# Performer attention and MLP: chunks of six token tiles with 384-column seven-product matmuls in place of chunks of four with 256- and 512-column ones

## The chip, the cores and the metric

The kernel runs on one core of one Trainium2 chip. The metric is the device time of one execution in microseconds (us), the median of several; lower is better. Engine names in the profile: PE is TensorE (matmul), PEld its weight loads, DVE VectorE, ACT ScalarE, POOL GpSimd, SP SyncE, from whose queue nearly all DMAs are started.

## The reference

Attention with random features (8 batches, 8 heads, 576 positions, 64 dimensions, 128 features), then a mixing step over the positions and an MLP over 512 channels. What the change touches is the last line but one, the MLP:

```python
q_s, k_s = q * scale, k * scale
q_p, k_p = phi(q_s), phi(k_s)              # exp(h - max h) / sqrt(m), h = x omega^T - |x|^2 / 2
kv = np.einsum('bhsm,bhsd->bhmd', k_p, v)
z = np.sum(k_p, axis=2)
attn = np.einsum('bhsm,bhmd->bhsd', q_p, kv) / (np.einsum('bhsm,bhm->bhs', q_p, z)[..., None] + 1e-6)
x = attn.transpose(0, 2, 1, 3).reshape(8, 576, 512)
h = x.transpose(0, 2, 1) @ U @ V
u = x + h.transpose(0, 2, 1)               # 4608 tokens x 512 channels
ch = np.maximum(u @ w_ch1, 0.0) @ w_ch2    # 512 -> 2048 -> 512
return u + ch
```

## The kernel before

The 4608 tokens are 36 tiles of 128. The attention and mixing stages write u to DRAM, by chunks of tiles (`u_dram`). The MLP reads it back chunk by chunk: `fetch` loads it by channel blocks into `uraw`, `turn` transposes these on VectorE into `uT` (128 channels x tokens). Since float32 products are built from reduced-precision ones, each operand is split: ScalarE casts the high part (line 814), VectorE or GpSimd subtracts it from the value to get the low part (line 815), and `passes` (high by high, high by low, low by high) makes three matmuls of each product. The splits of the layer-1 weights w1 (`wx`, made from `w1f`) are computed once, by ScalarE and GpSimd, and stored to `wx_dram`; later chunks load them (`Again`, line 874). A chunk goes through two layers:

- Layer 1 makes the hidden features, in feature tiles of 128, by tokens in the columns. `whole1` (line 963) does it directly: 4 channel blocks x 3 passes for each feature tile. `products` (line 1041) takes two feature tiles, two halves of the channels and two halves of the tokens as a 2 x 2 block product and does it with seven products instead of eight (Strassen-Winograd): seven sums of token blocks (`us`, `total`) and seven sums of weight blocks are multiplied, and `near` and `far` in SBUF collect sums of the products (`add` and `sums`, line 822; ScalarE's copies, line 1001). `relu` (lines 972 and 976) writes the high and low part of the hidden features, `g`.
- Layer 2, `second` (line 1087), multiplies `g` by w2, one 512-column matmul for each token tile, feature tile and pass, into one PSUM bank for each token tile (`p_n`, `p_q`, in chunk 0 `p_m` and `p_kv` too). It is a generator: `take` interleaves its matmuls with those of layer 1 of the next features. `store` (lines 1108, 1109) adds the residual row `u`, loaded by `residual` (line 1103), and sends the sum out.

The chunks before: chunk 0 has six tiles and uses `whole1` in 512 + 256 columns; chunks 1 to 7 have four tiles and use `products`, with token halves of 256 columns; the last has two tiles and uses `whole1` in 256 columns. A pass is one pair of feature tiles; eight passes make a chunk (sixteen for `whole1`). In chunk 1 the six matmuls of a product have 256 columns and alternate with layer-2 matmuls. In chunks 2 to 7 passes are wide: the weight's high part is multiplied by the operand's high and low part side by side (one matmul of 512 columns for each half of the channels), its low part by the high part alone (256), in groups of products (0, 1), (2, 3), (4, 5), (6); the last pass of each chunk is narrow as in chunk 1.

Operands for the next chunk are made in the last passes of the chunk before (`between` calls `nxt.prepare` and `nxt.add`), in eight buffers that go round: `ux` (six) and `uy` (two), of 2 channel blocks x high and low x 256. `keep_in_program_order` fixes the order of the instructions of the MLP on each engine as the code states them; DMAs stand in SP's queue in the order of the code, each behind what it waits for.

## Time and profile before

| | us |
|---|---|
| median of 3 runs | 1078.26 (1077.96 to 1078.32) |
| the profiled execution's own time | 1078.48 |
| span of the profile | 1076.6 |
| PE busy | 1066.3 (99%) |
| DVE busy | 769.9 (72%) |
| ACT busy | 530.3 (49%) |
| POOL busy | 308.1 (29%) |
| start of chunk 0's whole pass, start of chunk 1's products | 306.9, 439.5 |
| end of the last matmul | 1072.7 |

Busy time is the time in which an engine had an instruction in work. The span runs from the first to the last recorded instruction; the execution's own time holds 1.9 us around it. Matmuls overlap in the records (one of 512 columns has a record of 0.39 us and starts 0.227 us after the one before), so prices are read from start to start, as the chain of waits has them. A window is a stretch in us from the span's start.

### The profile page before, as it was taken

The page shows a single profiled execution, that of the slowest core. Times are in us where ns is not written, and L with a number is a line of the kernel's source. Part 1 is how long each engine was busy: PE and PEld are TensorE (multiplying, and loading weights), DVE is VectorE, ACT ScalarE, POOL GpSimd, SP SyncE. Part 2 cuts the span into 40 slices and gives each one's busy share as a digit, 9 for nine tenths or more (in the row PEclk, how much of TensorE's full clock was granted, in tenths as well). Part 3 has the DMA queues.
Part 4 walks back from the last instruction along what each step waited for, and adds up shares of the span by engine and source line. Part 5 has one row for each costly group of instructions (what it writes and reads, how often), then busy time and mean ns, then how long its engine had stood idle before and what let it go on. Part 6 is the DMA issues. An engine that isn't in the chain of part 4 may idle for free.

```text
span 1076.6 us, 19792 instructions
## 1 busy us (share of the span) xinstructions
PE 1066.3 (99%) x6517; PEld 944.5 (88%) x6517; DVE 769.9 (72%) x1781; ACT 530.3 (49%) x1503; POOL 308.1 (29%) x325
## 2 busy tenths in 40 slices
PE   8999999999999999999999999999999999999998
PEld 7999999999988888888888888888888888888887
DVE  4798998998987776655766767677676676766621
ACT  4899989898856664443322322322322322322332
POOL 3347448556445556565200000000000000000143
PEclk9999999999999999999999999999999999999999
DMA  8899989797224553565775785785685686586410
GB/s 134 146 164 153 180 165 159 166 183 122 80 91 144 143 151 92 201 214 197 259 234 176 231 239 185 206 257 184 193 272 184 196 254 203 183 238 205 147 60 20
DMA packets 346662, 188.73 MB, mean 175 GB/s; under 512 B 278208, under 2 KB 278208, under 8 KB 346560
## 3 DMA queue, kind: packets, MB, share of 16 engines
q1 hardware_dynamic: 344192, 187.17, 66.1%
q8 instruction: 53, 0.87, 0.4%
q10 hardware_dynamic: 2368, 0.30, 0.2%
q14 instruction: 49, 0.40, 0.1%
HBM read 153.85 MB, written 33.55 MB: 174 GB/s over the span
## 4 chain that ended last, share of the span: by engine, by line
PE 85%; DVE 6%; ACT 3%; issue 2%; POOL 2%; DMA 2%; SPq 0%; POOLq 0%; DVEq 0%; ACTq 0%
PE p_s L1041 25%; PE p_n L1087 18%; PE p_q L1087 15%; PE p_p L963 5%; PE p_kv L485 4%; PE p_n L531 4%; PE p_p L573 3%; PE p_p L574 3%; PE p_p L575 3%; PE p_q L511 2%; PE py L345 2%; DMA kt<-in_k_dram 1%; DVE mag L160 1%; POOL mag L182 1%; DVE nm L581 1%
## 5 line engine op out<-in xcount | busy, mean ns | idle before, releaser
L1041 PE MATMUL p_s<-ux,wx 128*128 128x256 f32 (+1 forms) x1282 | 265.2, 319 | 0.6 <-DVE far L822 0.4
L1041 PEld LDWEIGHTS p_s<-ux,wx 128*128 128x128 f32 x1282 | 227.0, 188 | 36.0 <-DVE far L822 0.7
L815 POOL TENSOR_TENSOR wx<-w1f,wx 128x256 fp32r<-128x256 f32 x86 | 68.5, 812 | 549.1 <-DMA u<-u_dram 494.8
L822 DVE TENSOR_TENSOR near<-p_s,near 128x256 f32<-128x256 f32 x383 | 161.6, 422 | 63.1 <-PE p_s L1041 51.9
L1087 PE MATMUL p_n<-w2h,g 128*128 128x512 f32 x576 | 199.1, 393 | 0.0
L1087 PE MATMUL p_q<-w2h,g 128*128 128x512 f32 x512 | 183.6, 393 | 0.0
L588 ACT ACTIVATE e<-p_p,nm 128x128 f32<-128x128 f32 x576 | 167.6, 390 | 23.7 <-DVE nm L581 15.1
L972 ACT ACTIVATE g<-far 128x256 fp32r<-128x256 f32 x112 | 46.8, 418 | 202.4 <-DVE far L822 202.4
L435 POOL TENSOR_TENSOR xl<-xT,xh 128x384 fp32r<-128x384 f32 x95 | 94.3, 1012 | 114.0 <-ACT xh L431 90.4
L1087 PEld LDWEIGHTS p_n<-w2h,g 128*128 128x128 f32 x576 | 108.7, 189 | 16.9
L581 DVE TENSOR_REDUCE nm<-p_p 128x4 f32<-128x512 f32 x144 | 97.8, 680 | 22.6 <-PE p_p L575 12.9
L1087 PE MATMUL p_n<-w2l,g 128*128 128x512 f32 x288 | 113.7, 395 | 0.0
L1087 PEld LDWEIGHTS p_q<-w2h,g 128*128 128x128 f32 x512 | 93.4, 189 | 13.7
L1041 PE MATMUL p_s<-uy,wx 128*128 128x256 f32 (+1 forms) x468 | 103.0, 317 | 0.0
L1087 PE MATMUL p_q<-w2l,g 128*128 128x512 f32 x256 | 100.2, 391 | 0.0
L1041 PEld LDWEIGHTS p_s<-uy,wx 128*128 128x128 f32 x468 | 84.6, 188 | 12.5
L573 PE MATMUL p_p<-omh,xh 128*128 128x256 f32 x288 | 92.8, 322 | 1.4 <-ACT e L588 0.9
L963 PE MATMUL p_p<-ux,wx 128*128 128x512 f32 (+1 forms) x480 | 84.5, 326 | 0.1
L963 PEld LDWEIGHTS p_p<-ux,wx 128*128 128x128 f32 x480 | 73.8, 190 | 9.2 <-DVE g L976 0.5
L574 PE MATMUL p_p<-oml,xh 128*128 128x256 f32 x288 | 81.6, 283 | 0.0
L575 PE MATMUL p_p<-omh,xl 128*128 128x256 f32 x288 | 81.5, 284 | 0.0
L822 DVE TENSOR_TENSOR far<-p_s,far 128x256 f32<-128x256 f32 x86 | 36.5, 425 | 60.1 <-ACT far L1001 58.7
(143 smaller groups left out, 1935.5 us busy)
## 6 DMA issues: line engine op xcount, KB each, us to landing
wx<-wx_dram SPq DMA_DIRECT2D x336, 256.0 KB, 3.0
raw<-in_moe_w_ch_dram SPq DMA_DIRECT2D x32, 512.0 KB, 4.0
wx_dram<-wx SPq DMA_DIRECT2D x56, 256.0 KB, 2.0
u_dram<-x SPq DMA_DIRECT2D x36, 256.0 KB, 2.2
u<-u_dram SPq DMA_DIRECT2D x34, 256.0 KB, 4.4
out_dram<-u SPq DMA_DIRECT2D x34, 256.0 KB, 3.4
qt<-in_q_dram SPq DMA_DIRECT2D x120, 72.0 KB, 2.9
kt<-in_k_dram SPq DMA_DIRECT2D x52, 144.0 KB, 4.9
```

Of the source, the lines that this page charges most:

```text
L435: rest.tensor_tensor(out=self.xl[-1], in0=self.turned, in1=f32(self.xh[-1]), op=ALU.subtract)
L573: nc.tensor.matmul(o, part.xh[g][:, ts], oh, start=True, stop=False)
L574: nc.tensor.matmul(o, part.xh[g][:, ts], ol, start=False, stop=False)
L575: nc.tensor.matmul(o, part.xl[g][:, ts], oh, start=False, stop=True)
L581: nc.vector.tensor_reduce(out=self.nm[:, :n], in_=self.pp[:, :n], axis=AX.X, op=ALU.max, negate=True)
L588: nc.scalar.activation(out=self.e[:, j, :], in_=self.pp[:, j, :], func=AF.Exp, bias=self.nm[:, j : j + 1])
L815: low = lambda: keep(rest.tensor_tensor(out=l, in0=x, in1=f32(h), op=SUBTRACT))
L822: keep(nc.vector.tensor_tensor(out=out, in0=a, in1=b, op=op))
L963: nc.tensor.matmul(ph, l, r, start=(cc + i == 0), stop=(cc == NC - 1 and i == 2))
L972: keep(nc.scalar.activation(out=g[:, 0, ts], in_=x, func=AF.Relu))
L1041: tc.keep_in_program_order(nc.tensor.matmul(to, l, r, start=(i in (0, 1, 2, 5) and first), stop=last, skip_group_check=True))
L1087: tc.keep_in_program_order(nc.tensor.matmul(po, l, r, start=(begin and n + i == 0), stop=(end and n == len(fs) - 1 and i == 2)))
```

## The change

- All chunks have six tiles (CT = 6), six chunks instead of nine: chunk 0 by `whole1` in two halves of 384 columns, chunks 1 to 5 by seven products with token halves of 384 columns, six matmuls of 384 for each product, no wide form. After each product a fixed count of layer-2 matmuls follows (`spread`).
- Each pass uses two PSUM banks for the seven products (X and Y of tag `p_p`) instead of four, so that `p_n`, `p_q`, `p_m` and `p_kv` hold the six sums of layer 2 in every chunk. Products 0 and 2, 1 and 3, 4 and 6 add up in one bank each, so the second of a pair waits until the first's sum has been read; the order of products and of the weight sums is changed for it.
- Operands lie in seven fixed buffers, `slots`, one for each product. Chunk 0's own operands are `slots` 0 to 3. An operand of the next chunk is made in the chunk's last pass, right after the product that used its slot. Chunk 1's transposed blocks stand in `early`, which has the buffers of slots 4 to 6; those of later chunks stand in w1's own space `w1f`, no longer needed then.
- Sums of token blocks for chunk 1 are GpSimd's, except `total(4)`; all lows of token operands are VectorE's. Weight splits stay with GpSimd.
- The residual rows of tiles 4 and 5 of a chunk take the buffers of tiles 0 and 1, so their loads stand behind these stores (`todo`).

The diff, cut to its core:

```diff
-    CT, TOK = 4, 4 * P
-    ends = [6, *range(10, NP * NT, CT), NP * NT]
+    CT, TOK, HT = 6, 6 * P, 3 * P
+    ends = list(range(CT, NP * NT + 1, CT))
...
+    slots = [uxp.tile([P, 2, 2, HT], F32R, name=f"ux{i}") for i in range(NC)]
...
+    slots += [None] * 3
+    early = [up.tile([P, 2, 2, HT], F32, name=f"ux{i}", bufs=1) for i in range(NC, 7)]
...
+        def block(self, d, t):
+            if self.c > 1:
+                return w1f[:, 2 * d : 2 * d + 2, t * DF // 2 : t * DF // 2 + HT]
+            return ((early[0][:, 0], early[0][:, 1]), (early[2][:, 0], early[1][:, 0]))[d][t]
+
+        def total(self, i):
+            if i == 3:
+                return self.block(0, 1)
+            if self.c > 1:
+                return w1f[:, 0:2, HT : 2 * HT] if i == 1 else w1f[:, 2:4, HT : 2 * HT]
+            if i == 2:
+                return early[1][:, 1]
+            if i not in self.sums:
+                self.sums[i] = late["rp"].tile([P, 2, HT], F32, name="uraw", bufs=2)
+            return self.sums[i]
...
-            op = self.slot(self.ops)
-            halve(op[:, :, 0], op[:, :, 1], x, nc.gpsimd if self.c == 1 and i in (3, 5) else nc.vector, pend)
-            if i == 1 and 4 not in self.s:
-                four = lambda: self.sum(4, blk(1, 0), self.s[2], SUBTRACT, self.s[2])
-                four() if pend is None else pend.append(four)
+            if self.c == 1 and i >= NC:
+                slots[i] = up.tile([P, 2, 2, HT], F32R, name=f"ux{i}", bufs=1)
+            split(slots[i], x, nc.vector)
+            self.made += 1
...
-            X, Y, Z, W = bank("p_p", 2), bank("p_p", 2), bank("p_m", 1), bank("p_kv", 1)
-            near = dec.tile([P, 4, HT], F32, name="near", tag="raw", bufs=RB)
-            far = dec.tile([P, 2, HT], F32, name="far", tag="de", bufs=2)
-            g = [gp.tile([P, 2, TOK], F32R, name="g", bufs=4) for _ in range(2)]
+            X, Y = bank(), bank()
+            (p1, u2), (u3, c21), (c22, c12) = (room() for _ in range(3))
+            g = {}
...
                 if i == 0:
-                    whole(p1, X)
+                    keep(nc.scalar.copy(out=p1, in_=X))
                 elif i == 1:
-                    add(u2, Y, p1)
+                    sums(u2, Y, p1, ADD)
                 elif i == 2:
-                    if wide:
-                        whole(c22, Z)
+                    g[0, 0] = self.relu(X)
                 elif i == 3:
...
+                    sums(u3, Y, p1, ADD)
                 elif i == 4:
...
+                    sums(c22, X, u3, ADD)
+                    g[1, 1] = self.relu(c22)
                 elif i == 5:
...
+                    sums(c21, Y, u3, ADD)
+                    g[1, 0] = self.relu(c21)
                 elif i == 6:
...
+                    sums(c12, X, u2, ADD)
+                    g[0, 1] = self.relu(c12)
+
+            for i in range(7):
+                if i == 4:
+                    X = bank()
+                o, x, wt = Y if i in (1, 3, 5) else X, slots[i], w.ops[i]
+                for k in range(2):
+                    for j, (l, r) in enumerate(passes((wt[:, 0, k], wt[:, 1, k]), (x[:, 0, k], x[:, 1, k]))):
+                        keep(nc.tensor.matmul(
+                            o, l, r, start=(i in (0, 1, 4, 5) and k + j == 0), stop=(k == 1 and j == 2),
+                            skip_group_check=True,
+                        ))
+                take(steps, spread[i])
+                after(i)
+                between(i)
...
+                if end:
+                    todo = [lambda t=t, po=po: self.store(t, po)]
+                    if self.c and t < 2:
+                        todo.append(lambda t=t: self.residual(t + 4))
+                    if self.c < NCH - 1:
+                        stores.extend(todo)
+                    else:
+                        for step in todo:
+                            step()
...
+                    if i == 3 and 2 <= p < 6:
+                        nxt.turn()
+                    if p == 6 and i in (1, 3, 5):
+                        nxt.prepare(i // 2 + 1)
+                    if p == 7:
+                        nxt.add()
+
+            spread = (3, 3, 3, 3, 2, 2, 2) if c == 1 and p == 0 else (5, 5, 5, 5, 5, 5, 6)
+            g = now.products(pairs, between, steps, spread)
             take(steps)
             pairs = new
             if p == NH - 1:
-                for t in range(CT):
+                for t in range(4):
                     now.residual(t)
...
-    g = nxt.whole1(ws.pop(0))
     take(steps)
-    while stores:
-        stores.pop(0)()
...
-    take(whole_pass(nxt, g, each))
```

Three places show how it moves instructions. Numbers behind names are those of buffers.

VectorE where chunk 0 ends, before, from chunk 0's last `relu` (`g` from `p_p`) on: `uy` and `ux` are lows of chunk 1's operands, `ws` sums of weight blocks, `near` the first sum of a product, the rows with `u` the adds of the stores.

```order
L976 SCALAR_TENSOR_TENSOR g_6740<-p_p_6727,g_6740 128x512
L976 SCALAR_TENSOR_TENSOR g_6756<-p_p_6743,g_6756 128x256
L815 TENSOR_TENSOR uy_6759<-us_6671,uy_6759 128x2x256
L822 TENSOR_TENSOR ws_6763<-w1f_75,ws_6614 128x256
L815 TENSOR_TENSOR ux_6778<-us_6669,ux_6778 128x2x256
L815 TENSOR_TENSOR ux_6797<-us_6673,ux_6797 128x2x256
L1108 TENSOR_TENSOR u_6667<-p_m_5641,u_6667 128x512
L815 TENSOR_TENSOR ux_6830<-uT_5532,ux_6830 128x2x256
L822 TENSOR_TENSOR near_6813<-p_s_6810,near_6813 128x256
```

The same place after, from the weight sum behind the last `relu` on; `ux0` to `ux6` are the slots, but `ux4_5399`, `ux5_5400` and `ux6_5401` are the early blocks in the same buffers.

```order
L809 TENSOR_TENSOR ws_6775<-w1f_72,ws_6612 128x256
L806 TENSOR_TENSOR ux0_87<-ux4_5399,ux0_87 128x768
L806 TENSOR_TENSOR ux1_88<-ux5_5400,ux1_88 128x768
L806 TENSOR_TENSOR ux2_89<-ux6_5401,ux2_89 128x768
L806 TENSOR_TENSOR ux3_90<-ux4_5399,ux3_90 128x768
L806 TENSOR_TENSOR ux4_6804<-uraw_6667,ux4_6804 128x768
L809 TENSOR_TENSOR ws_6811<-w1f_72 128x256
L809 TENSOR_TENSOR ws_6813<-ws_6811,w1f_72 128x256
L809 TENSOR_TENSOR near_6791<-p_s_6790,near_6791 128x384
L1036 TENSOR_TENSOR u_6685<-p_n_5635,u_6685 128x512
L809 TENSOR_TENSOR uraw_6831<-ux6_5401,ux5_5400 128x768
L806 TENSOR_TENSOR ux6_6833<-ux5_5400,ux6_6833 128x768
```

Behind the last `relu` there stand seven lows of 768 columns and `total(4)` (`uraw_6831`) with the first sums and stores between them (the seventh low, `ux5_6854`, is three rows on), where there were four lows of 512, three of them ahead of the first store.

TensorE in a middle pass, before: a wide group of two products (its 512s, then its 256s), then layer-2 matmuls by `w2h` and `w2l`.

```order
L1041 MATMUL p_s<-ux,wx 128x512 x4
L1041 MATMUL p_s<-ux,wx 128x256 x4
L1087 MATMUL p_n<-w2h_5619,g 128x512
L1087 MATMUL p_n<-w2l_5620,g 128x512
L1087 MATMUL p_n<-w2h_5619,g 128x512
L1087 MATMUL p_n<-w2h_5635,g 128x512
```

After, products of chunk 5's last pass:

```order
L991 MATMUL p_s<-ux_90,wx 128x384 x6
L1012 MATMUL p_q<-w2h_5631,g 128x512
L1012 MATMUL p_q<-w2l_5632,g 128x512
L1012 MATMUL p_q<-w2h_5631,g 128x512
L1012 MATMUL p_q<-w2h_5615,g 128x512
L1012 MATMUL p_q<-w2l_5616,g 128x512
L991 MATMUL p_s<-ux_6804,wx 128x384 x6
```

Each product now stands alone, six matmuls of 384 columns, five of layer 2 behind it.

SP's queue at the program's end, before: the four stores of the last chunk of four, the residual rows of the last two tiles, their stores. DMAHW names a DMA that must have landed, DVE a VectorE instruction.

```order
L1109 DMA out_dram<-u 128x512 [waits DMAHW6_49,DVE_49]
L1109 DMA out_dram<-u 128x512 [waits DMAHW7_49,DVE_49]
L1103 DMA u<-u_dram_74 128x512 [waits DMAHW4_49,DMAHW0_49]
L1103 DMA u<-u_dram_74 128x512 [waits DMAHW5_49,DMAHW1_49]
L1109 DMA out_dram<-u 128x512 [waits DMAHW2_49,DVE_49]
L1109 DMA out_dram<-u 128x512 [waits DMAHW3_49,DVE_49]
```

After: the six stores of the last chunk, with two loads between them.

```order
L1037 DMA out_dram<-u 128x512 [waits DMAHW4_49,DVE_49]
L1031 DMA u<-u_dram_71 128x512 [waits DMAHW5_49,DMAHW4_49]
L1037 DMA out_dram<-u 128x512 [waits DMAHW6_49,DVE_49]
L1031 DMA u<-u_dram_71 128x512 [waits DMAHW7_49,DMAHW6_49]
L1037 DMA out_dram<-u 128x512 [waits DMAHW0_49,DVE_49]
L1037 DMA out_dram<-u 128x512 [waits DMAHW1_49,DVE_49]
```

Each load waits for the store ahead of it to land (the second semaphore it names), and the next store is queued behind the load.

## Rows read from the trace of the kernel before

**Rows 1.** The page: busy time by engine, granted clock in 40 slices

```profile
PE 1066.3 (99%) x6517; PEld 944.5 (88%) x6517; DVE 769.9 (72%) x1781; ACT 530.3 (49%) x1503; POOL 308.1 (29%) x325
...
PEclk9999999999999999999999999999999999999999
```

**Rows 2.** Windows (width, busy and count by engine, PEclk): chunk 0, then the rest

```profile
306.90:439.52 132.62, 132.35 (x671) 112.57 (x670) 94.52 (x146) 73.11 (x151) 67.88 (x66) 1.00 0.47 133
439.52:1072.73 633.21, 632.65 (x3401) 545.35 (x3399) 412.78 (x978) 193.12 (x509) 75.31 (x90) 1.00 0.65 199
```

**Rows 3.** The chain near the end: start, us, engine, tile, line, matmuls

```profile
1026.35 2.72 PE p_q L1087 x12
1029.07 1.43 PE p_p L963 x12
1030.50 1.39 PE p_n L1087 x6
```

**Rows 4.** Windows of line 1041, of line 1087; line 1041's 512-column groups

```profile
439.52:1072.73 633.21, 350.02 (x1750) 308.26 (x1749) 1.00 0.65 199
...
439.52:1072.73 633.21, 412.76 (x1459) 261.86 (x1458) 1.00 0.65 199
...
L1041 PE MATMUL p_s<-ux,wx 128*128 128x512 f32 x446 | 124.9, 390 | 0.0
...
L1041 PE MATMUL p_s<-uy,wx 128*128 128x512 f32 x156 | 45.8, 389 | 0.0
```

**Rows 5.** Windows of one wide pass and of one pass of chunk 1

```profile
655.68:666.05 10.37, 10.37 (x53) 8.79 (x53) 7.36 (x19) 2.58 (x7) 0.00 (x0) 1.00 0.57 178
476.49:486.99 10.50, 10.50 (x68) 9.45 (x67) 5.49 (x14) 4.20 (x13) 6.08 (x7) 1.00 0.47 175
```

**Rows 6.** TensorE's timeline in chunk 1's first pass: start us, us, instruction

```profile
447.21 1.95 PE L1041 MATMUL p_s<-ux,wx 128*128 128x256 f32 x12
```

**Rows 7.** Groups by form (busy, mean ns): from chunk 1; last two, chunk 0

```profile
L822 DVE TENSOR_TENSOR near<-p_s,near 128x256 f32<-128x256 f32 x383 | 161.6, 422 | 63.1 <-PE p_s L1041 51.9 <-ACT near L1001 1.8
...
L1108 DVE TENSOR_TENSOR u<-p_n,u 128x512 f32<-128x512 f32 x17 | 11.7, 687 | 5.4 <-PE p_n L1087 5.4
L815 DVE TENSOR_TENSOR ux<-uT,ux 128x512 fp32r<-128x512 f32 x16 | 11.6, 724 | 2.3 <-ACT ux L814 2.2
...
L814 ACT CAST ux<-uT 128x512 fp32r<-128x512 f32 x16 | 9.9, 618 | 3.6 <-PE p_s L1041 3.6
...
L814 ACT CAST wx<-w1f 128x256 fp32r<-128x256 f32 x29 | 10.4, 402 | 0.0
L976 DVE SCALAR_TENSOR_TENSOR g<-p_p,g 128x512 fp32r<-128x512 f32 x14 | 9.7, 692 | 22.7 <-ACT g L972 22.7
```

**Rows 8.** The page's weight splits; the timeline ahead of chunk 1

```profile
L815 POOL TENSOR_TENSOR wx<-w1f,wx 128x256 fp32r<-128x256 f32 x86 | 68.5, 812 | 549.1 <-DMA u<-u_dram 494.8
...
436.60 0.69 DVE L815 TENSOR_TENSOR uy<-us,uy 128x512 fp32r<-128x512 f32 x1
...
437.55 2.94 DVE L815 TENSOR_TENSOR ux<-us,ux 128x512 fp32r<-128x512 f32 x2
...
437.38 1.42 POOL L923 TENSOR_TENSOR us<-uT,us 128x512 f32<-128x512 f32 x1 [6.87 <-DVE uy L815]
438.75 1.19 POOL L815 TENSOR_TENSOR wx<-ws,wx 128x256 fp32r<-128x256 f32 x1
```

**Rows 9.** The end: timeline, the chain's last step, DMAs from 1028 us

```profile
1072.34 0.39 PE L1087 MATMUL p_n<-w2h,g 128*128 128x512 f32 x1
1072.80 1.02 SPq L1109 DMA_DIRECT2D out_dram<-u  x2
...
1072.76 0.69 DVE u L1108
...
out_dram<-u SPq DMA_DIRECT2D x4, 256.0 KB, 2.1
u<-u_dram SPq DMA_DIRECT2D x2, 256.0 KB, 2.8
```

More of the change, by code (lines that the diff above doesn't have):

```diff
@@ L938, in add, with prepare @@
-        def add(self, pend=None):
-            i, blk = len(self.ops), self.block
+        def prepare(self, i):
+            a, b = {
+                1: lambda: (self.block(0, 1), self.block(0, 0)),
+                2: lambda: (self.block(1, 1), self.total(1)),
+                3: lambda: (self.block(1, 1), self.block(0, 1)),
+                4: lambda: (self.block(1, 0), self.total(2)),
+            }[i]()
+            sums(self.total(i if self.c == 1 or i < 4 else 2), a, b, SUBTRACT, nc.gpsimd if self.c == 1 and i < 4 else nc.vector)
@@ L1010, in after, with products, bank, room @@
+        def products(self, w, between, steps, spread):
+            def bank():
+                return ps.tile([P, HT], F32, name="p_s", tag="p_p", bufs=2)
+            def room():
+                t = dec.tile([P, 2 * DM], F32, name="near", tag="raw", bufs=RB)
+                return t[:, :HT], t[:, HT : 2 * HT]
+            X, Y = bank(), bank()
+            (p1, u2), (u3, c21), (c22, c12) = (room() for _ in range(3))
+            g = {}
             def after(i):
                 if i == 0:
-                    whole(p1, X)
+                    keep(nc.scalar.copy(out=p1, in_=X))
@@ L1221, in between @@
                     pairs.add()
[L1222 removed]
+                if new and len(pairs.ops) == 7:
                     new.add()
```

313 lines of the change are left out of this document (77 added, 236 removed).

## Prediction

> **What bounds the kernel now.** I read the page's totals first. TensorE is busy 1066.3 of 1076.6 us and its granted clock stays in the top tenth (2.4 GHz) in every slice, while VectorE is at 72% [rows 1]. The windows say where: the whole pass of chunk 0 is 132.35 us busy of 132.62, and all that follows, seven-product chunks and tail, 632.65 of 633.21 [rows 2]. So the time of these stages is the sum of their matmuls, plus the few places where an operand is late, plus what stands behind the last matmul. Three things can move it: what the matmuls cost, new stalls of TensorE, and the tail. Everything is summed against the profiled execution, 1078.48 us (span 1076.6), which lies 0.2 above the median of 1078.26.
>
> **What a matmul costs.** The chain at the end gives it start to start: 12 matmuls of 512 columns in 2.72 us, 226.7 ns each; 12 of 256 in 1.43 us, 119.2 ns, and 120 without the first [rows 3]. Both lie on columns/2.4 + 13.3 ns. The 384-column form is not in the trace. By that line it costs 173.3 ns; in proportion to the 512 form it would be 170.0; I take the line, since two measured widths lie on it.
>
> The Trainium skill ("TensorE: Matmul & The Clock Gate", section "Back-to-back issue gap") gives an isolated gap of N/2.4 + 2.5 ns. With 2.5 in place of 13.3 the saving worked out next would be 3.2 us instead of 6.05. These rows show 226.7 where it has 216, so the row decides.
>
> **Matmuls from chunk 1 on.** Before, line 1041 has 1750 there, 446 + 156 = 602 of 512 columns and so 1148 of 256; the whole pass of the last two tiles adds 16 × 12 = 192 of 256 to make 1340; layer 2 has 1458 of 512 (the row counts one over the edge) [rows 4]. That is 602 × 226.7 + 1340 × 120 + 1458 × 226.7 = 627.8 us. After, five chunks × eight passes × 42 = 1680 matmuls of 384 and the same layer 2: 1680 × 173.3 + 1458 × 226.7 = 621.7. **−6.05 us**: 6144 columns fewer (the last two tiles now go through seven products instead of eight) are 2.56, and 262 matmuls fewer × 13.3 ns are 3.5. In chunk 0 nothing moves: per feature tile 24 × 173.3 = 4.16 us against 12 × 226.7 + 12 × 120 = 4.16.
>
> **Switching between widths.** A wide pass of before, 38 matmuls of 512 and 14 of 256, is 10.30 us by these prices and takes 10.37 [rows 5]: 0.02 us for each of its four switches. A pass of chunk 1, where narrow and wide alternate all the time, takes 10.50 against 42 × 120 + 24 × 226.7 = 10.48 [rows 5]: nothing. The chunks of before pay 43 wide passes × 0.075 = 3.2 us, and the 15 passes of the tail 15 × 0.03 (1.39 for six instead of 1.36 [rows 3]) = 0.4, in all 3.6. After, 5 × 8 × 7 = 280 products of six 384s each stand between layer-2 steps; at 0 to 0.02 us they cost 0 to 5.6. As 384 lies between the form that costs nothing and the one that costs 0.02, I take the middle, 2.8: **−0.8 us**.
>
> **Stalls that go.** In chunk 1's first pass, 12 matmuls take 1.95 us at 447.21, where 12 × 0.12 = 1.44 and some 0.16 of overlap at the last would stand: a stall of 0.35 [rows 6]. In all, the window's 633.21 less 627.8 and 3.6 leaves 1.8. I let 1.3 go, since those stood in chunk 1's order, which is rewritten: **−1.3 us**.
>
> **The first seven-product pass.** This is the part with the largest cost. Before, operands 0 to 3 of chunk 1 were split into buffers of their own, in part while chunk 0 still ran; VectorE had only four 512-wide lows left around the last whole pass. After, slots 0 to 3 are chunk 0's own operands, so all four 768-wide lows stand behind chunk 0's last layer-1 matmul, and slots 4 to 6 are the buffers of the early blocks, so operand 4 can be cast only when low 3 has read its block, and operand 6 only when the sum `total(4)` has read its own. VectorE and ScalarE form one chain. Durations for the new widths are put on straight lines: the 256-wide add takes 422 ns and the 512-wide 687 [rows 7], so 0.56 for 384, 0.95 for 768; low 724 at 512 [rows 7], so 0.97 to 0.99; cast 402 and 618 [rows 7], so 0.83; the second ReLU step 692 at 512 [rows 7], so 0.56. Successive VectorE instructions overlap by some 0.08.
> With W the end of that matmul: ReLU 0.5 and its low 0.56 to 1.1, a weight sum to 1.5, four lows to 5.1, and about 1.2 for splits of GpSimd beside them: low 3 at 6.3. Cast 4 to 7.1, low 4 to 8.1, two weight sums to 9.5, `u2` at about 10.2; the store add to 10.8, `total(4)` to 11.7, cast 6 to 12.6, low 6 to 13.5, a wait on ScalarE and the ReLU low of product 2 to 14.7. TensorE has 18 layer-2 matmuls (4.1 us) to cover the start and then wants product i at 4.1 + 1.73·i (six 384s and three 512s): product 3 at 9.3, but its bank waits for `u2`: 1.0. Product 4 would be at 12.0, but takes the bank that the ReLU low of product 2 frees: 2.7. Then 0.7 for product 5 and 0.1 for product 6, behind low 5 and its neighbours, and 0.7 + 0.4 at the next pass, whose first products wait for the last adds. Sum 5.6; I take **+5.5 us**. The lower bound is 4 (no time lost to GpSimd). The upper one: GpSimd makes eight weight splits there, 812 ns each [rows 8], 6.5 us in all. Before, VectorE's two lows at 437.55 took 2.94 us, 1.5 each, while GpSimd's sum and split ran at 437.38 and 438.75; the one at 436.60, with GpSimd idle, took 0.69 [rows 8]. Were all the splits to stand in the chain, 5.5 − 1.2 + 6.5 gives about 10.
> This trace agrees with a rule that speaks against the change: the Trainium skill ("SBUF — State Buffer", section "Who interferes with whom") says that a VectorE instruction with two SBUF inputs contends with a GpSimd instruction that reads SBUF, one of them blocked for the other's whole length.
>
> **Boundaries between later chunks.** Four times, in the last pass, VectorE makes operands 0 to 6 of the next chunk beside the adds and ReLU lows. From product 4 of that pass I count add, ReLU low, low 4 (0.97), add, ReLU low, `total(4)` (0.95), low 5, add, with two casts between: 17.7 to 18.1 us after the pass began. Product 1 of the next chunk wants it at 17.65. So 0.1 to 0.5 each; I take 0.2, **+0.8 us** (0 to 2). Elsewhere VectorE has room: 7.36 of 10.37 us in a wide pass [rows 5], and after that fewer, wider instructions, since two banks need no adds across halves.
>
> **The tail.** Before, the last matmul ends at 1072.73 (1072.34 + 0.39), its add runs 1072.76 to 1073.45, and the span ends at 1076.6, 3.9 us behind the matmul [rows 9]. Stores of the quiet end land 2.1 us after issue, loads 2.8 [rows 9]. After, tiles 4 and 5 of the last chunk get their residual into the buffers of tiles 0 and 1, so SP's queue runs store 0, load 4 (waits for store 0 to land), store 1, load 5 (waits for store 1), then the others. Tiles are six 512s, 1.36 us, apart. With E the last matmul's end: tile 0 is added at E − 6.1, its store lands at E − 4.0, store 1 is issued by E − 3.6 (issues 0.5 us apart: 1.02 for two [rows 9]) and lands at E − 1.5, load 5 lands at E + 1.4, the add ends at E + 2.1, and the 3.15 us from the add to the end of the span follow: 5.25, or 5.9 if every issue costs its 0.5 again. **+1.4 to +2.0; I take +1.7.** Before, this cost nothing, as the two tail tiles had their rows early.
>
> The attention stage has the same instructions, with a few places interchanged: 0 ± 0.7.
>
> **Sum.** −6.05 − 0.8 − 1.3 + 5.5 + 0.8 + 1.7 = −0.15 on 1078.48, and 0.2 lower against the median: **1078.1 us**, no change that can be measured (0.2%, 2.2 us, is about what a measurement of this kernel can tell).
>
> **Rivals.** A, faster: 384-column switches cost nothing (−2.8) and the first pass stalls for only 4 us (−1.5): 1073.8. For it: chunk 1's alternation cost nothing [rows 5]. Against: the long runs of 512s behind a change of width paid 0.02.
>
> A2: 384 costs 170.0 ns: 2064 × 3.3 ns = −6.8: 1071.3. Against it: the line through 256 and 512.
>
> B, slower: VectorE and GpSimd lock each other out through the first pass, stall 10: 1082.6. It decides from 7.7 us of stall (1080.3). For it: the 1.5 us lows [rows 8]. Against: the splits can fall into the chain's ScalarE steps. The page on SBUF cited above is this rival's rule.
>
> C: the fixed cost per matmul is 2.5 ns, so fewer matmuls bring less: 1078.1 + 2.85 = 1081. Against: both widths of [rows 3]. It is the rule of the page on TensorE cited above.
>
> **How the numbers follow.** Forecast 0.46, A 0.24, A2 0.06, B 0.22, C 0.02. Of the forecast's own spread (1076.0 to 1080.5, from the middle bounds of switches, boundaries and tail) nearly all lies within 0.2%; A and A2 are faster, with 0.02 of the forecast; B and C slower by most of theirs, some 0.21. So faster 0.32, same 0.46, slower 0.22. The range reaches to A and B: 1073.0 to 1082.6.
>
> **What would show it.** Right: six 384s at 1.04 us between layer-2 runs of five 512s, a pass of 42 × 173.3 + 36 × 226.7 ns = 15.4 us plus at most 0.14 for its switches; TensorE idle some 5 us in the first pass of chunk 1, longest behind the ReLU low of product 2, and almost nowhere after; 5.3 to 5.9 us between the last matmul's end and the end of the span. Wrong: six 384s at other than 1.03 to 1.05 us, idle time of TensorE at the start of every chunk or inside its middle passes, or a granted clock at the lower level behind the new waits.

## The result: 1086.76 us, slower by 0.8%

| | before | after |
|---|---|---|
| median, us | 1078.26 | 1086.76 (1086.72 to 1087.0) |
| span of the profile | 1076.6 | 1084.9 |
| start of chunk 0's whole pass | 306.9 | 306.1 |
| start of chunk 1's products | 439.5 | 439.8 |
| end of the last matmul | 1072.7 | 1078.6 |
| from there to the end of the span | 3.9 | 6.3 |

The ratio is 1.008, with a 95% interval of 1.0057 to 1.0103. The forecast, 1078.1, was wrong, and so was the range, 1073.0 to 1082.6. Of the 8.3 us that the span grew, −0.8 lie ahead of the whole pass, +1.1 in it, +5.6 between the first product and the last matmul, and +2.4 behind it.

### The profile after

The page of the changed kernel: busy time by engine, and the clock granted to TensorE. It answers [rows 1].

```profile
span 1084.9 us, 18047 instructions
...
PE 1069.6 (99%) x6255; PEld 977.2 (90%) x6255; DVE 656.3 (60%) x1311; ACT 478.0 (44%) x1273; POOL 274.0 (25%) x286
...
PEclk9999999999999999999999999999999999999999
```

There are 262 matmuls fewer, and yet TensorE is busy for 3.3 us longer; VectorE's load has fallen from 72% to 60%, at no gain. The clock is at its upper level throughout.

Windows of the same two stretches as [rows 2], then one pass of chunk 3: width, busy time and count of PE, PEld, DVE, ACT and POOL, clock, DMA share, GB/s.

```profile
306.13:439.81 133.68, 133.10 (x671) 120.51 (x670) 95.22 (x148) 72.83 (x149) 69.05 (x65) 1.00 0.50 140
439.81:1078.62 638.81, 635.72 (x3139) 570.18 (x3137) 298.48 (x506) 141.69 (x282) 40.22 (x50) 1.00 0.51 148
...
700.04:715.79 15.75, 15.75 (x79) 14.19 (x79) 7.42 (x13) 2.54 (x5) 0.00 (x0) 1.00 0.84 252
```

The second stretch was forecast at 621.7 us of matmuls, 2.8 of switches between widths, 6.3 of new stalls and the 0.5 of old ones that were left in place, 631.3 in all. It takes 638.81. The middle pass shows where the excess is: 15.75 us without idle time, where 42 × 173.3 + 36 × 226.7 ns make 15.44. The chain of that stretch (start, us, what), with neither stall nor wait in it:

```profile
709.13 1.16 PE p_n L1012 x5
710.28 1.06 PE p_s L991 x6
711.35 1.16 PE p_n L1012 x5
712.50 1.06 PE p_s L991 x6
```

Six 384s take 1.06 us where 1.04 were forecast, and five 512s 1.16 where 1.133 were; over all 280 groups (a run of 384s and the 512s behind it) the mean is 0.044 us more for each. I summed the starts of all matmuls from the first product on, less the straight prices (120, 173.3 and 226.7 ns), and counted gaps above 25 ns as stalls. What is left I call the **surcharge**. Before, it is 3.9 us (−2.9 at the 256s, +6.8 at the 512s) with 1.3 of stalls; after, 12.4 us (+6.55 at the 384s, +5.88 at the 512s) with 4.5 of stalls. So −6.05 + 8.5 + 3.2 = 5.7 us, against the 5.6 that the windows show.

TensorE's waits after, from chunk 1 on (us in total, times, longest):

```profile
PE p_s L991 <- DVE g L948: 1.8, 1, 1.8
PE p_s L991 <- DVE near L809: 1.3, 3, 0.7
```

All of these lie between 445 and 459 us, in the first pass of chunk 1 and the start of the second; later chunks have none above 0.03 us. VectorE's timeline there (start, us, instruction; idle time before it and its releaser in brackets):

```profile
437.80 4.05 DVE L806 TENSOR_TENSOR ux<-ux,ux 128x768 fp32r<-128x768 f32 x4
442.75 0.96 DVE L806 TENSOR_TENSOR ux<-uraw,ux 128x768 fp32r<-128x768 f32 x1 [0.90 <-ACT ux L805]
443.63 0.97 DVE L809 TENSOR_TENSOR ws<-w1f 128x256 f32<-128x256 f32 x1
444.63 0.84 DVE L809 TENSOR_TENSOR ws<-ws,w1f 128x256 f32<-128x256 f32 x1
445.39 0.54 DVE L809 TENSOR_TENSOR near<-p_s,near 128x384 f32<-128x384 f32 x1
...
448.30 0.96 DVE L806 TENSOR_TENSOR ux<-ux,ux 128x768 fp32r<-128x768 f32 x1 [0.90 <-ACT ux L805]
449.18 0.55 DVE L948 SCALAR_TENSOR_TENSOR g<-p_s,g 128x384 fp32r<-128x384 f32 x1
```

This is the chain of the prediction: four lows behind chunk 0's last layer-1 matmul (about 435.9), a cast waited for, low 4, two weight sums, `u2` done at 445.93, the cast behind `total(4)`, low 6, and the ReLU low of product 2 done at 449.73. Product 4 starts at 449.78, the 1.8 us wait.

The tail after, by the chain that ended last, answers [rows 9]:

```profile
1074.55 0.02 issue
1074.58 0.44 DVE u L1036
1075.02 3.06 DMA out_dram<-u
1078.07 0.02 issue
1078.09 2.91 DMA u<-u_dram
...
1081.12 0.69 DVE u L1036
```

The add of tile 5 runs at 1081.12, 2.5 us behind the last matmul: it waited for store 1 to land (3.06 us) and for its residual row (2.91 us).

### The profile page after: what moved, and what is told of

Its sections match the earlier page's. It is cut to its first block, busy times and chain, and to the rows that moved or that the text cites. A ratio compares the mean times of both kernels' runs of the same rounds, so it can differ in the third digit from the quotient of the medians.

```text
span 1084.9 us, 18047 instructions
## 1 busy us (share of the span) xinstructions
PE 1069.6 (99%) x6255; PEld 977.2 (90%) x6255; DVE 656.3 (60%) x1311; ACT 478.0 (44%) x1273; POOL 274.0 (25%) x286
## 4 chain that ended last, share of the span: by engine, by line
PE 91%; DVE 3%; ACT 2%; DMA 1%; issue 1%; POOL 1%; SPq 0%; DVEq 0%; ACTq 0%; POOLq 0%
PE p_s L991 27%; PE p_n L1012 12%; PE p_q L1012 12%; PE p_p L939 6%; PE p_kv L1012 6%; PE p_m L1012 6%; PE p_kv L486 4%; PE p_n L532 4%; PE p_p L574 3%; PE p_p L575 3%; PE p_p L576 3%; PE p_q L512 2%; PE py L346 2%; ACT e L589 1%; DVE nm L582 1%
## 5 line engine op out<-in xcount | busy, mean ns | idle before, releaser
L991 PE MATMUL p_s<-ux,wx 128*128 128x384 f32 x1680 | 343.3, 339 | 3.1 <-DVE g L948 1.8
L991 PEld LDWEIGHTS p_s<-ux,wx 128*128 128x128 f32 x1680 | 305.0, 188 | 28.2 <-DVE near L809 3.2
L809 DVE TENSOR_TENSOR near<-p_s,near 128x384 f32<-128x384 f32 x200 | 111.3, 556 | 179.9 <-PE p_s L991 179.8
L947 ACT ACTIVATE g<-near 128x384 fp32r<-128x384 f32 x120 | 63.0, 525 | 281.9 <-DVE near L809 281.8
L1012 PE MATMUL p_q<-w2h,g 128*128 128x512 f32 x384 | 135.0, 392 | 0.0
L1012 PE MATMUL p_n<-w2h,g 128*128 128x512 f32 x384 | 128.8, 392 | 0.0
L948 DVE SCALAR_TENSOR_TENSOR g<-near,g 128x384 fp32r<-128x384 f32 x120 | 67.1, 559 | 71.0 <-ACT g L947 71.0
L532 PE MATMUL p_n<-kv,eT 128*128 128x65 f32 x512 | 71.2, 269 | 0.1
L939 PE MATMUL p_p<-ux,wx 128*128 128x384 f32 x384 | 71.0, 336 | 0.0
L532 PEld LDWEIGHTS p_n<-kv,eT 128*128 128x128 f32 x512 | 67.1, 192 | 2.3 <-DVE x L557 0.3
```

The source lines that it names most:

```text
L532: nc.tensor.matmul(pn[:, h, :], eT[:, h, :], kv[:, h, s // 5, :], start=True, stop=True)
L809: keep(engine.tensor_tensor(out=out, in0=a, in1=b, op=op))
L939: keep(nc.tensor.matmul(ph, l, r, start=(cc + i == 0), stop=(cc == NC - 1 and i == 2)))
L947: keep(nc.scalar.activation(out=g[:, 0], in_=x, func=AF.Relu))
L991: keep(nc.tensor.matmul(o, l, r, start=(i in (0, 1, 4, 5) and k + j == 0), stop=(k == 1 and j == 2), skip_group_check=True,))
L1012: keep(nc.tensor.matmul(po, l, r, start=(begin and n + i == 0), stop=(end and n == len(fs) - 1 and i == 2)))
```

## The experiments

Four parts of the sum were open: the surcharge, the first pass, the boundaries and the tail. The theory formed from the two traces was that each change of the matmuls' width costs time, spread over the next five or six matmuls. The rivals were that the change between layers costs it, or that a 384-column matmul is simply dearer than its straight price. Most numbers below stand on the stretch from a kernel's first product to its last matmul, so that the attention stage, whose end moves between 305.8 and 308.1 us from kernel to kernel, doesn't blur it. The two latest ends, 308.1 in e6 and 307.5 in e11, follow a stretch at the lower clock level early in that stage (e6: 0.51 granted from 28.5 to 35.4 us). The runs also come from several chips, on which the kernel before took 1077.4 to 1079.4 us, so a microsecond between two runs' times is not read as an effect.

### e1_tail

```diff
-            if self.c == 0 and t in (2, 3):
+            if t in ((2, 3) if self.c == 0 else (4, 5)):
                 self.u[t] = dec.tile([P, DM], F32, name="u", tag="de", bufs=2)
...
-                    if self.c and t < 2:
-                        todo.append(lambda t=t: self.residual(t + 4))
...
-                for t in range(4):
+                for t in range(CT):
                     now.residual(t)
```

> The residual rows of tiles 4 and 5 of chunks 1 to 5 get two buffers of their own and are loaded with the other four, so no load stands between the stores at the end. In the changed kernel 6.28 us lie between the end of the last matmul (1078.62) and the end of the span (1084.9), 3.87 in the kernel before. Theory (the reload is on the path): the last add follows its last matmul at once, about 3.9 us are left, the time falls by 2.4 us. Rival (the six stores one behind the other set the end): 5 us or more stay, the time falls by 1 us at most.

It took 1084.1 us with a span of 1082.3, 2.6 below the changed kernel. The chain at its end:

```profile
1077.11 1.37 PE p_kv L1012 x6
1078.48 0.02 issue
1078.51 0.69 DVE u L1034
```

The last add follows its matmul at once, and 3.9 us are left behind the matmul, as in the kernel before. The reload was the whole of the tail's loss.

### e2_l2_384

```diff
-                            po, l, r, start=(begin and n + i == 0), stop=(end and n == len(fs) - 1 and i == 2)
+                            po[:, :HT], l, r[:, :HT], start=(begin and n + i == 0), stop=(end and n == len(fs) - 1 and i == 2)
...
-            keep(nc.vector.tensor_tensor(out=u, in0=po, in1=u, op=ALU.add))
+            keep(nc.vector.tensor_tensor(out=u[:, :HT], in0=po[:, :HT], in1=u[:, :HT], op=ALU.add))
```

> Layer 2 is done for 384 of its 512 output columns only (the last 128 output channels are left out, and get no MLP part), so that all matmuls of both layers from chunk 0 on have 384 columns; the alternation of the layers, their operands, banks and waits stays as it was. In the changed kernel, from chunk 1's first product on, a run of six 384s costs 23 ns over 6 x 173.3 and a run of five 512s 20 ns over 5 x 226.7, in all 12.4 us. Theory (each change of width costs, spread over the next five or six matmuls): with one width both runs lie on 173.3 +- 1 ns for each matmul, the total over it below 1 us. Rival (the change from one layer to the other costs, whatever the width): the 384s of layer 1 still cost 177 on average, some 12 us in all. The span falls by 53.4 ns for each of 1728 layer-2 matmuls, 92 us, and by 12 more by the theory.

The span is 994.4 us. Its chain in a middle pass:

```profile
703.43 1.04 PE p_s L991 x6
704.48 0.87 PE p_m L1012 x5
705.34 1.04 PE p_s L991 x6
706.38 1.04 PE p_kv L1012 x6
```

Six matmuls take 1.04 us in either layer, five take 0.87: 173.3 ns for each, without a trace of the change of layer. Over 3137 matmuls the surcharge is 0.2 us. So neither the alternation nor the 384 form itself costs anything, and both of those rivals fall: it is the meeting of two widths. (With layer 2 shorter, VectorE was late more often, and stalls rose to 11.5 us; the surcharge doesn't count them. With 5.8 us that chunk 0 did not give back and 1.5 at the tail, they are why the span fell by 90.5 us and not by the 104 expected.)

### e3_pairs

```diff
-            for i in range(7):
+            for group in ((0, 1), (2, 3), (4, 5), (6,)):
+                for i in group:
...
-                take(steps, spread[i])
-                after(i)
-                between(i)
+                take(steps, sum(spread[i] for i in group))
+                for i in group:
+                    after(i)
+                    between(i)
```

> Products are done in groups (0, 1), (2, 3), (4, 5), (6), each group followed by the layer-2 matmuls that stood behind its products: the same matmuls, but 160 groups in place of 280. Theory (cost for each change of width): a long run of 384s costs 26 ns and one of 512s 30 over the straight price (as in chunk 0), so 160 x 56 ns = 9.0 us in place of 12.4, the time falls by 3.4 us. Rival (a 384-column matmul simply costs 177): 12.4 us stay. Stalls of the first pass and of chunk boundaries may change by up to 1 us either way.

The surcharge fell as expected, to 9.4 us, but the time rose to 1090.32: stalls went from 4.5 to 11.35 us. About 1.2 us of this stands at each of the four chunk starts, as product 1 now follows product 0 directly and waits for VectorE's last adds: the profile names no releaser, but at the first of them the add that reads product 1's bank ends at 569.31, and product 1 starts at 569.42. About 1.5 us are no wait at all. The window from the restart behind the longest stall (TensorE idle for 2.0 us) on:

```profile
446.28:450.46 4.18, 4.18 (x14) 3.59 (x15) 3.28 (x5) 2.67 (x5) 1.47 (x2) 0.62 0.08 31
```

In it the granted clock averages 0.62, and 512s start 0.42 us apart: the lower level, 1.2 GHz, for most of these 4 us. e2 shows the same behind its longest stall (1.9 us idle), and e9 behind 2.0 us. e12, also with 1.9 us idle, does not, so no limit can be read from these runs. In the changed kernel, where TensorE's longest wait at the same place is 1.8 us, no such stretch follows.

### e4_fine

```diff
                             skip_group_check=True,
                         ))
-                take(steps, spread[i])
+                        if 3 * k + j < spread[i]:
+                            take(steps, 1)
```

> The layer-2 matmuls of a product stand one by one between its 384s (384, 512, 384, 512 and so on) instead of in a run behind them, as in chunk 1 of the kernel before: the same matmuls, five times as many changes of width. Theory in its plain form (every change costs some 22 ns): the cost over the straight prices rises from 12.4 to about 60 us, +48. Theory in its other form (the cost builds up over the five or six matmuls behind a change and a lone matmul pays only its first share, +4 and +2 ns): about 9 us, -3.4. If neighbours even out as in chunk 1 of before: near 0, -12.

1097.63 us; the surcharge is 18.8 us, none of the three forms. The chain, one matmul after the other:

```profile
702.38 0.23 PE p_n L1013
702.61 0.18 PE p_s L991
702.79 0.24 PE p_q L1013
703.02 0.18 PE p_s L991
```

A lone 512 between 384s costs 236 ns instead of 226.7, a 384 about 176 instead of 173.3: 12 ns for a pair of changes, not 44 and not 0. The cost is therefore neither a price for each change nor one that only long runs pay; in runs of five and six it had built up to about four times that of a lone pair. Stalls were 9.1 us here, since products end later.

### e5_first

```diff
-            if self.made == 5:
+            if self.made == (4 if self.c == 1 else 5):
                 self.prepare(4)
...
-                if new and len(pairs.ops) == 7:
+                if new and len(pairs.ops) == 7 and (c, p, i) != (1, 0, 0):
                     new.add()
```

> With the tail of e1 kept (so 2.4 us less there), two edits in the first seven-product pass, on the chain of VectorE and ScalarE that was named as its limit: total(4) is made ahead of the low of operand 4 (in the time in which VectorE waits for ScalarE's cast), and the two weight sums that stood ahead of u2 are made at the end of the pass. Theory (this chain sets the stalls of 0.9 us at product 3 and 1.9 at product 4): u2 comes 1.8 us earlier and the ReLU low of product 2 some 3 us earlier, both stalls go, and of 4.5 us from chunk 1 on 1 to 1.5 are left; TensorE's last matmul ends 3 us earlier than in e1 (1078.47), at about 1075.4. Rival (GpSimd's splits hold VectorE, whatever the order): the stalls move but 3.5 us or more remain. The cost of the changes of width stays at 12.4 us.

1081.69 us, the last matmul at 1076.07, surcharge 12.4, stalls 2.4 instead of 4.5. The order of VectorE's work was thus worth 2.2 us of the first pass, not 3. Its waits:

```profile
PE p_s L991 <- DVE near L809: 0.6, 2, 0.4
PE p_s L991 <- ACT near L968: 0.4, 1, 0.4
```

The long wait for the ReLU low is gone; shorter ones, behind stores and weight sums further on in the same queue, took part of its place. The two weight sums also came at another time, with no GpSimd split beside them, and took less; the first:

```profile
445.41 0.41 DVE L809 TENSOR_TENSOR ws<-w1f 128x256 f32<-128x256 f32 x1
```

### e6_two_runs and e7_two_runs_pool

```diff
             spread = (3, 3, 3, 3, 2, 2, 2) if c == 1 and p == 0 else (5, 5, 5, 5, 5, 5, 6)
+            if p != NH - 1 and (c, p) != (1, 0):
+                spread = (0, 0, 0, 18, 0, 0, 18)
```

> e5 with the layer-2 matmuls of a pass in two runs of 18 (behind products 3 and 6) instead of seven, in all passes but the first of chunk 1 and the last of each chunk: 110 groups in place of 280, 68 of them long. Theory (each change of width costs some 26 to 30 ns in all, however long the run behind it): 68 x 0.056 + 42 x 0.044 = 5.6 us in place of 12.4, the last matmul ends 6.8 us earlier than in e5. Rival (the cost grows with the number of 384s): 12 us stay. Products 4 and 6 now stand close behind those whose sums they wait for: theory expects no stall above 0.1 us, since 1.04 us lie between, or 4.1 of layer 2.

e7 has the second line without `p != NH - 1`, and:

```diff
-            split(slots[i], x, nc.vector)
+            split(slots[i], x, nc.gpsimd if self.c > 1 and i in (2, 4) else nc.vector)
```

> e6 with the two runs of 18 in the last pass of each chunk too (80 groups in all but 7 long), and the low parts of operands 2 and 4 of chunks 2 to 5 made by GpSimd, which is idle there, instead of VectorE. Theory: 73 long groups x 0.056 + 7 x 0.044 = 4.4 us for changes of width; VectorE's chain at the four boundaries is 2 us shorter, so the tighter last pass costs no more than 0.5 us at each boundary; the last matmul ends 1 us earlier than in e6. Rival (VectorE and GpSimd block each other, 1.5 us for a low instead of 0.7 as seen ahead of chunk 1 of the kernel before, and the operands come late): 1 to 2 us at each boundary, 4 to 8 us later than e6.

1088.55 and 1086.71 us. From the first product to the last matmul e6 takes 641.0 us and e7 641.4, e5 636.6; that e6's time is the longer one comes from its attention stage, the one with the lower clock level, which ended some 2 us later. The surcharge fell to 6.9 and 6.0 us, but stalls rose to 12.3 and 13.6, more than the gain. The waits of e6 from chunk 1 on:

```profile
PE p_s L991 <- issue: 3.9, 4, 1.0
PE p_s L991 <- ACT near L968: 2.8, 5, 1.5
PE p_s L991 <- DVE near L809: 1.6, 3, 1.0
```

"issue" is time for which the profile shows no releaser. Nearly all of this stands where products follow each other without layer 2 between while operands or weights are still being made: 3.4 us in chunk 1's second pass, 1.8 at each later chunk's start. In the middle passes there is none. In e7 the two lows on GpSimd took 1.93 and 1.84 us in each last pass. VectorE's lows stood beside the first for 0.2 to 0.3 us only and took 0.95 and 1.12. Beside the second there was a ReLU low of VectorE, first VectorE's row, then GpSimd's:

```profile
563.00 1.40 DVE L948 SCALAR_TENSOR_TENSOR g<-near,g 128x384 fp32r<-128x384 f32 x1 [0.59 <-ACT g L947]
...
562.15 1.84 POOL L806 TENSOR_TENSOR ux<-w1f,ux 128x768 fp32r<-128x768 f32 x1 [5.93 <-ACT ux L805]
```

Its neighbours with GpSimd idle took 0.56 us; this one took 1.40 and ended 0.4 behind GpSimd's low. So the block of the rival is there, 0.8 us of it on an instruction that the expectation had not counted. Its loss of 4 to 8 us against e6 did not come, 0.4 did. TensorE waited 4.6 us for VectorE's adds, among them 0.9 in each last pass, where the long runs stood now too.

### e8_mid_runs

```diff
+            spread = (5, 5, 5, 5, 0, 10, 6)
+            if c == 1 and p < 2:
+                spread = (5, 5, 5, 5, 5, 5, 6) if p else (3, 3, 3, 3, 2, 2, 2)
+            elif 0 < p < NH - 1:
+                spread = (0, 0, 0, 18, 0, 0, 18)
```

> e5 with the two runs of 18 only where e6 had no stall with them: passes 1 to 6 of chunks 2 to 5 and 2 to 6 of chunk 1; the first and the last pass of a chunk keep seven runs, but products 4 and 5 stand together. That is 126 groups, 58 of them long. e6 gives the price of a long group, (6.9 - 42 x 0.044)/68 = 0.074 us, dearer than the 0.056 of chunk 0. Theory: 58 x 0.074 + 68 x 0.044 = 7.3 us for changes of width in place of 12.4, stalls as in e5 (2.4 us), the last matmul ends at 1076.07 - 5.1 = 1071.0, and the time is 5.1 us below e5's 1081.69, about 1076.6, which would be below the kernel before. Rival (the stalls of e6 at chunk starts come from the middle passes, whose sums end later with long runs): 1.6 us at each of four chunk starts, no better than e5.

1077.25 us (1076.69 to 1077.81), with a ratio to the kernel before of 0.999 (0.998 to 1.0). The surcharge is 7.4 us, stalls 2.5, and the last matmul ends at 1071.05, all as the theory had it; the median lies 0.65 above the expected 1076.6. Its middle pass by the chain:

```profile
703.52 4.20 PE p_s L991 x24
707.72 2.76 PE p_n L1012 x12
...
711.84 3.14 PE p_s L991 x18
```

24 matmuls of 384 at the straight price are 4.16 us, 18 are 3.12, 12 of 512 are 2.72: a surcharge of 0.04, 0.02 and 0.04 for a whole run. The starts, summed by a matmul's place in its run, show where it lies. In runs of eighteen 384s the first six pay 26 ns together and the twelve behind them nothing; in runs of eighteen 512s the first nine pay 41 and the nine behind them nothing. The runs of 24 pay some 14 more, at their last six, for which no run shows a reason. In the kernel before, where they follow 256s, long runs of 512s pay 27 ns in their first five and nothing behind. So a change of width is paid for within the next six to nine matmuls, and a run of five 512s, as in the changed kernel, ends when it has paid 20 of the 41.

### e9_l1_256 and e12_l1_320

```diff
-                return ps.tile([P, HT], F32, name="p_s", tag="p_p", bufs=2)
+                return ps.tile([P, HT], F32, name="p_s", tag="p_p", bufs=2)[:, : 2 * P]
...
-                            o, l, r, start=(i in (0, 1, 4, 5) and k + j == 0), stop=(k == 1 and j == 2),
+                            o, l, r[:, : 2 * P], start=(i in (0, 1, 4, 5) and k + j == 0), stop=(k == 1 and j == 2),
...
-                ts = slice(t % 3 * P, (t % 3 + 1) * P)
+                m = t % 3 if self.c == 0 else min(t % 3, 1)
+                ts = slice(m * P, (m + 1) * P)
```

> The changed kernel with 256 of the 384 columns of each token half in the products of chunks 1 to 5 (the third token tile of each half is left out, and layer 2 takes the second one's features for it): the same 280 groups of six and runs of five 512s, only the narrow matmuls have 256 columns. If 256 behaves as in the wide passes of the kernel before, its runs gain 7 ns and the runs of five 512s lose 20 to 27: 280 x 0.015 = 4 us over the straight prices of 120 and 226.7. Theory (384 is a width of its own: its runs lose 24 ns where those of 256 gain 7): 3 to 6 us in place of 12.4. Rival (the order of the changed kernel, runs of six and five alone, costs 44 ns for each group whatever the narrow width): 12 us.

e12 is the same with 320 in place of 2 * P.

> As e9 (the changed kernel with narrower products: part of each token half left out, layer 2 takes the second tile's features for the third), with 320 columns in place of 256. Straight price 320/2.4 + 13.3 = 146.7 ns. In e9 1680 matmuls of 256 stood 2.1 us below and 1457 of 512 7.5 us above their straight prices, 5.4 in all; in the changed kernel those of 384 6.6 above and those of 512 5.9, 12.4 in all. If the surcharge runs evenly with the width, 320 gives 9 us in all, 2 of it at the narrow ones. If 384 alone is dear: 5 to 6. If every width but 256 is dear: 12 or more.

The chains in a middle pass, first of e9:

```profile
701.40 0.71 PE p_s L991 x6
702.11 1.16 PE p_q L1013 x5
703.27 0.71 PE p_s L991 x6
```

and of e12:

```profile
701.46 0.88 PE p_s L991 x6
702.33 1.16 PE p_n L1013 x5
703.49 0.88 PE p_s L991 x6
```

Same groups, same runs, same layer 2, same buffers: the surcharge is 5.4 us with 256 columns (−2.1 at the narrow ones, +7.5 at the 512s) and 5.4 with 320 (−1.45 and +6.8), against 12.4 with 384 (+6.55 and +5.9). A run of five 512s pays 20 to 27 ns whatever stands before it. The narrow runs are what differs: six 256s or 320s take a little less than the straight price (0.71 for 0.72, 0.875 for 0.88), six 384s 0.024 more. It doesn't run evenly with the width; of the three, 384 alone is dear next to 512.

### e10_best and e11_best

e10 against e8:

```diff
-                for _ in range(2):
+                for _ in range((0, 0, 1, 1, 1, 1, 1)[i] if (c, p) == (1, 0) else 2):
                     if stores:
...
-                if new and len(pairs.ops) == 7 and (c, p, i) != (1, 0, 0):
+                if new and len(pairs.ops) == 7 and not ((c, p) == (1, 0) and i < 3):
...
-            elif 0 < p < NH - 1:
+            elif p == 0:
+                spread = (5, 5, 0, 8, 0, 0, 18)
+            elif p < NH - 1:
                 spread = (0, 0, 0, 18, 0, 0, 18)
```

> e8 with two edits. In the first pass of chunk 1 the stores start two products later and stand one behind each product, and the next weights are made from product 3 on, so that the ReLU low of product 2 and the adds behind products 3 to 5 come earlier on VectorE; and the first pass of chunks 2 to 5 has its layer-2 matmuls as 5, 5, 8 and 18 in place of six runs. Theory: of the 2.5 us of stalls left in e8, all in the first pass and the start of the second, 1.0 to 1.5 go; 8 groups fewer give 0.3 to 0.4 off the changes of width (7.4 in e8); the last matmul ends at about 1069.3 in place of 1071.05, the time is 1.5 to 1.9 us below e8, about 1075.5. Rival: the weights of the second pass, made later, now stall TensorE there by as much, and the time stays at e8's 1077.25.

1077.35 us, as e8: the rival held. The eight groups fewer gave nothing either: the surcharge is 7.5 us, in e8 7.4. The first pass has one stall left (0.5 us), but the second now has one of 1.5 at 457.98. ScalarE's timeline ahead of it:

```profile
456.22 0.71 ACT L805 CAST wx<-ws 128x256 fp32r<-128x256 f32 x2 [1.56 <-DVE ws L809]
456.84 0.40 ACT L805 CAST wx<-w1f 128x256 fp32r<-128x256 f32 x1
457.14 0.40 ACT L805 CAST wx<-ws 128x256 fp32r<-128x256 f32 x1
457.45 0.47 ACT L968 COPY near<-p_s 128x384 f32<-128x384 f32 x1
```

The copy of product 0, for which product 2 waits, stands behind four casts of weights, and these behind a weight sum of VectorE.

e11 against e10:

```diff
-                    if i == 6:
+                    if i == 6 and (c, p) != (1, 0):
                         while len(new.ops) < 7:
```

> e10, but the weights of products 4 to 6 of chunk 1's second pass are made in that pass, one behind each product, instead of all at the end of the first. In e10 the 1.5 us stall at 457.98 waits for ScalarE's copy of product 0, which stood in ScalarE's queue behind casts of these weights. Theory: that stall goes, 0.5 to 0.9 us of stalls are left from chunk 1 on, the time is 1.3 to 1.7 us below e10: 1075.8, 0.2% below the kernel before. Rival: the weights come too late for products 4 to 6 and TensorE waits for GpSimd's splits there, 1 us or more: 1077.

1076.52 us (1075.87 to 1078.04) beside 1078.43 of the kernel before on the same chip: a ratio of 0.9981 (0.9972 to 0.999), so it beats both kernels, the one before by 0.2%. The 1.5 us stall fell to 0.6, but two new ones of 0.3 came at 472 us: stalls are 2.2 us in all, barely less than in e10 (2.3), so the theory's 1.3 us within this stretch did not come. From the first product to the last matmul it takes 631.40 us, e10 631.56, e8 631.74, the kernel before 633.21. That is the gain that can be placed; how much of the 0.8 us by which e11's median lies below e10's is the edit and how much the chip stays open.

## Why the prediction was wrong

**The step that failed is "Switching between widths".** It was put at −0.8 us and measured +8.5: 3.9 paid before (3.6 forecast), 12.4 after (2.8 forecast, 5.6 at most). That is 9.3 us too little, where the whole forecast was 8.7 too low; the other terms nearly cancel. The sign of being wrong that the prediction names, six 384s at other than 1.03 to 1.05 us, is there: 1.06. The argument was that 384 lies between 256, which cost nothing when it alternated, and 512, which cost 0.02 us behind a change. Both rows were right [rows 3, 5], but neither bounds the new case. The row that cost nothing has its matmuls one by one, not in runs: e9 shows that the very order of the changed kernel would have cost 5.4 us with 256 columns, the upper end of the forecast. And the 0.02 us was the balance of two runs, 27 ns more at the 512s and 7 less at the 256s. The bracket took for granted that the cost lies between these two rows for a width between them. With 384 columns the 512s pay 20 ns, no more than before, but the narrow run, which used to give 7 ns back, pays 24 itself. Two runs at 0.02 us for each group, 280 × 0.04 = 11 us, would have put a rival at 1086.5, next to the 1086.76 measured.

Why a run of 384s next to 512s pays what 256s and 320s don't was not settled. The runs show that it isn't the layer (e2), nor 384 alone (e2), nor the order of runs (e9), and that it ends within a run, behind the sixth 384 and the ninth 512 (e8).

The other terms:

- **What a matmul costs** held: 173.3 ns for 384 in long runs (e2), so rival A2's 170.0 falls. The −6.05 us are in the sum. The rival of a 2.5 ns fixed cost falls too: 262 matmuls fewer brought what 13.3 ns give.
- **Stalls that go**: 1.3, as forecast.
- **The first seven-product pass**: 5.5 forecast, 4.5 measured, at the places named: 1.0 at product 3 was 0.9, 2.7 at product 4 was 1.9 by the matmuls' starts. `u2` was forecast at 10.2 us behind chunk 0's last layer-1 matmul and came at 10.0; the ReLU low of product 2 at 14.7 and came at 13.8. e5 confirms the chain by taking 2.2 us off it through its order alone. Rival B, 10 us, did not come. GpSimd's share came at other places than counted: of the four lows only the first stood beside a split and took 1.44 us, the others 0.95; three weight sums ahead of `u2` stood beside splits and took 0.88, 0.97 and 0.84, where two of them without a split beside them (e5) took 0.41 and 0.42. Together these are some 1.9 us on the way to `u2`, 0.5 of them at the lows, for which 1.2 had been counted; the 5.3 more that rival B adds up from all the splits did not come. That `u2` came within 0.2 us is thus in part luck. The Trainium skill's rule ("SBUF — State Buffer", section "Who interferes with whom"), that a VectorE instruction with two SBUF inputs contends with a GpSimd instruction that reads SBUF, is borne out by the 1.44 us low and the 0.84 to 0.97 us weight sums.
- **Boundaries between later chunks**: 0.8 forecast, nothing above 0.03 us each measured. The margin that was counted was there, but it is small: e3, e6 and e7 moved products closer to the chunk's start and met 0.9 to 1.8 us at each.
- **The tail**: +1.7 forecast, +2.4 measured, by the mechanism named (e1). Store 1 took 3.06 us to land and not 2.1; the row of the quiet end [rows 9] was too kind, while a load was in flight beside it here; whether that is the reason wasn't tried.
- **Chunk 0**: forecast unchanged, +1.1. Some 0.7 of it is the same surcharge (one change to 384s and back for each of its 15 feature tiles, at 67 ns in place of 21); the rest is a gap at its start, 0.75 us in place of 0.33, where TensorE waits for GpSimd's `ml` of the mixing step.

The rivals told the wrong story too: the slower one was put on VectorE and GpSimd, and the loss came from TensorE itself, which never looked idle.

## What to carry to other kernels

A price per matmul read from long runs of one width holds inside such runs only. Before a kernel is changed to a new width that alternates with another, count the runs, and charge both sides of each change at the dearest price seen; where many small groups alternate, gather them: the same matmuls in 2 long runs instead of 7 short ones gave back 5 us here. Longer runs take away the cover of the work that feeds them, so leave the short ones where operands are being made (the first and the last pass of a chunk), and give the last tiles of a program their inputs before the stores begin.

## What the runs showed of the hardware

- TensorE next to 512-column matmuls: six 384s cost 24 ns over 6 × 173.3, six 320s and 256s 5 to 8 ns less than their straight price; five 512s behind them 20 to 27 more. In long runs it ends: eighteen 384s pay 26 ns, all in the first six, and eighteen 512s behind 384s 41, all in the first nine (e8). One width throughout costs nothing (0.2 us over 3137 matmuls in e2).
- Straight prices from start to start lie on columns/2.4 + 13.3 ns at four widths: 120 (256), 146.7 (320, by the last two of each six in e12), 173.3 (384), 226.7 (512).
- VectorE beside GpSimd: a weight sum took 0.84 to 0.97 us beside a split and 0.41 to 0.42 without one (changed kernel, e5), a ReLU low with both inputs in SBUF 1.40 beside a GpSimd low and 0.56 without (e7).
- TensorE idle for 2.0 us was followed by a stretch of some 4 us, most of it at the lower clock level (e3: 0.62 granted on average, 512s 0.42 us apart), which cost about 1.5 us on top of the wait itself. The level fell behind waits of 1.9 us (e2) and 2.0 (e9) too, and stayed behind 1.9 us in e12 and 1.8 in the changed kernel.
